# A wide last tile in a fused retention and feed-forward kernel, and a reserve of work kept back for it

## Chip, cores, metric

One core of one Trainium2 chip. The metric is device time in microseconds (us) of one execution; most executions of one kernel agree within 0.3%. TensorE is called PE, VectorE DVE, ScalarE ACT, GpSimd POOL; the queue that issues all DMAs here is SyncE's (SPq).

## The reference

```python
def _attn_ref(q, k, v):                  # q, k, v: (4, 8, 768, 64), float32
    gamma = 1.0 - 2.0 ** (-5.0 - np.arange(H))
    for t in range(S):
        state = gamma * state + outer(k[:, :, t], v[:, :, t])
        y[:, :, t] = q[:, :, t] @ state / sqrt(D)

def _moe_ref(x, w1, w2, w3, w_out):      # x: (3072, 512) from y; w1, w2: (512, 1024)
    a = x @ w1
    b = x @ w2
    return (a * b @ w3) @ w_out          # (3072, 512)
```

The kernel computes the first part in 24 steps of 128 tokens and multiplies w3 and w_out once, so that the second part is a product (a), a product (b), their elementwise product and one more product (O) for each tile of tokens.

## The kernel before

A step does the scores of its 128 tokens, the state, and the outputs. Between these, a queue of units of the feed-forward part fills PE. The key reaches a step in three moves: a load, a transpose by DMA (into kT), and two copies by ACT into the layout that the scores read (kp). A tile of 256 tokens gives 16 a and b units (4 matmuls of 256 columns each, 0.44 us) and two O units (8 matmuls of 512 columns, 1.73 us). Cuts are marked.

```python
        def a_unit(self, f, tag=None):
            ps = self.mm(W1, f, tag)                       # 4 matmuls into a PSUM buffer, one of 3
            self.pa[f] = fsb.tile([128, TB], FP, tag="pa", name="pa", bufs=5)
            nc.scalar.copy(self.pa[f][:, :], ps[:, :])     # ACT frees the buffer

        def b_unit(self, f):
            ...
            ps = self.mm(W2, f)
            nc.vector.tensor_tensor(                       # DVE frees the buffer, and needs pa
                self.HT[:, f : f + TB // self.width, :].rearrange("p f n -> p (f n)"),
                self.pa.pop(f)[:, :], ps[:, :], MULT,
            )
...
        for i in range(0, len(units), 8):                  # a b a b a b a b O a b a b a b a b O
            fill.units += units[i : i + 8] + late[:1]
            late = late[1:]
...
    def step(n):
        ready = n * C
        share = fill.available(ready) / (2 - n % 2)
        casts(n + 2)                                       # POOL, cut: only n >= 4
        scores(n)
        fill.pull(share * 0.25, ready)
        t_new = kv(n)
        dma_transposes(n + 2)
        load_chunk(n + 4)
        ...
        fill.pull(share * 0.25, ready)
        outputs(n)
        Tst[0] = t_new
        transposes(n + 1)                                  # two ACT copies of the key into kp
        fill.pull(share * 0.5, ready)
```

Loads, transposes by DMA and stores of the output are all issued on one in-order queue.

Of the kernel before, what the change touches and what calls it, by code (L numbers as in the profile page):

```python
# [9 lines left out]
FP = mybir.dt.float32  # L10
HP = mybir.dt.float16
AF = mybir.ActivationFunctionType
MULT = mybir.AluOpType.mult
# [5 lines left out]
def kernel(  # L19
# [11 lines left out]
    nc = tc.nc  # L31
    B, H, S, D = q.shape
    C = 128
    WST = 12
    NCH = S // C
    NSTEP = B * NCH
    NTOK = B * S
    DT0 = 6
    NP = H // 2
    DM = 512  # L40
# [7 lines left out]
    wstage = ctx.enter_context(tc.tile_pool(name="wstage", bufs=WST))  # L48
    xpool = ctx.enter_context(tc.tile_pool(name="xpool", bufs=4))
    ld = ctx.enter_context(tc.tile_pool(name="ld", bufs=6))  # L50
    att = ctx.enter_context(tc.tile_pool(name="att", bufs=2))
    fsb = ctx.enter_context(tc.tile_pool(name="fsb", bufs=2))
# [3 lines left out]
    ps_f = ctx.enter_context(tc.tile_pool(name="ps_f", bufs=3, space=PSUM))  # L56
# [154 lines left out]
    for h in range(H):  # L211
        p, r = h // 2, (h % 2) * 64
        nc.gpsimd.memset(GS[r : r + 64, p, r : r + 64], gam[h] ** C)

    XT = {}
# [6 lines left out]
    W3O = [wpool.tile([128, DM], HP, name=f"w3o_{i}") for i in range(8)]  # L222
# [19 lines left out]
    def bank(tag, shape, dtype, name):  # L242
        return (ps_t if tag == "psT" else ps_at).tile(shape, dtype, tag=tag, name=name)
# [89 lines left out]
    def casts(n):  # L333
        if n >= NSTEP:
            return
        k32, v32 = chunk_in.pop(n)
        if n % 2 == 0:
            q_cast(n // 2)
        k16 = att.tile([128, 512], HP, tag="k16", name="k16", bufs=3)
        nc.gpsimd.tensor_copy(k16[:, :], k32[:, :])  # L340
        vp = VP[n % 3]

        for r in range(2):
            nc.gpsimd.tensor_tensor(  # L344
                vp[:, :, r, r * 64 : r * 64 + 64],
                v32[:, :].rearrange("j (p s e) -> j p s e", s=2, e=64)[:, :, r, :],
                VS[:, :].rearrange("j (p s) -> j p s", s=2)[:, :, r].unsqueeze(2).broadcast_to((128, NP, 64)),
                MULT,
            )
        k16s[n] = k16  # L350

    def q_transposes(m, later=False):

        if m >= DT0 // 2:
            return
# [25 lines left out]
    def by_dma(n):  # L381

        return n >= DT0 and n != DT0 + 1

    def dma_transposes(n):

        if n < DT0 or n >= NSTEP:
            return
# [11 lines left out]
    def queries(n, p):  # L400
        if n < DT0:
            return qTs[n][:, p, :]
        c = n % 2
        return qTd[n // 2][:, :, p, c * 64 : (c + 1) * 64]
# [67 lines left out]
    def outputs(n, tag="psY"):  # L472
        am, vp = ATs.pop(n), VP[n % 3]
        c = n % NCH
        ps = bank(tag, [128, NP, 128], FP, "psY")
        for p in range(NP):
            nc.tensor.matmul(ps[:, p, :], lhsT=vp[:, p, 0, :], rhs=am[:, p, 0, :], start=True, stop=False)  # L477
            nc.tensor.matmul(ps[:, p, :], lhsT=vp[:, p, 1, :], rhs=am[:, p, 1, :], start=False, stop=(c == 0))  # L478
            if c > 0:
                nc.tensor.matmul(ps[:, p, :], lhsT=Tst[0][:, p, :], rhs=queries(n, p), start=False, stop=True)  # L480
        if n % 2 == 0:
            XT[n // 2] = xpool.tile([128, NP, 256], HP, tag="xt", name="xt")

        order = "p a (t i) -> p a t i"
        nc.vector.tensor_tensor(  # L485
            XT[n // 2][:, :, n % 2 * C : (n % 2 + 1) * C].rearrange("p a (i t) -> p a t i", t=2),
            ps[:, :, :].rearrange(order, t=2), YS[:, :, :].rearrange(order, t=2), MULT,
        )


    TB = 256

    class Ffn:
        def __init__(self, tok0, width):
            self.tok0, self.width = tok0, width
            self.HT, self.pa = None, {}

        def mm(self, W, f, tag=None):

            if tag:  # L500
                ps = bank(tag, [128, TB], FP, "psG")
            else:
                ps = ps_f.tile([128, TB], FP, tag="psF", name="psF")
            w, c0 = self.width, self.tok0 % TB
            m = TB // w
            for i in range(m):
                for d in range(4):
                    nc.tensor.matmul(  # L508
                        ps[:, i * w : (i + 1) * w], lhsT=W[d][:, (f + i) * 128 : (f + i + 1) * 128],
                        rhs=XT[self.tok0 // TB][:, d, c0 : c0 + w],  # L510
                        start=(i == 0 and d == 0), stop=(i == m - 1 and d == 3),
                    )
            return ps

        def a_unit(self, f, tag=None):
            ps = self.mm(W1, f, tag)
            self.pa[f] = fsb.tile([128, TB], FP, tag="pa", name="pa", bufs=5)
            nc.scalar.copy(self.pa[f][:, :], ps[:, :])  # L518

        def b_unit(self, f):  # L520
            if self.HT is None:
                self.HT = fsb.tile([128, 8, self.width], HP, tag="ht", name="ht", bufs=3)
            ps = self.mm(W2, f)
            nc.vector.tensor_tensor(  # L524
                self.HT[:, f : f + TB // self.width, :].rearrange("p f n -> p (f n)"),
                self.pa.pop(f)[:, :], ps[:, :], MULT,
            )

        def o_unit(self, tb, between=None):
            psO = ps_f.tile([128, DM], FP, tag="psF", name="psO")  # L530
            for f in range(8):
                if f == 4 and between:
                    between()
                nc.tensor.matmul(  # L534
                    psO[:, :], lhsT=self.HT[:, f, tb * 128 : (tb + 1) * 128], rhs=W3O[f][:, :],
                    start=(f == 0), stop=(f == 7),
                )
            osb = fsb.tile([128, DM], FP, tag="osb", name="osb", bufs=3)
            nc.scalar.activation(osb[:, :], psO[:, :], AF.Copy, scale=final_scale)  # L539
            r0 = self.tok0 + tb * 128  # L540
            nc.sync.dma_start(out[r0 : r0 + 128, :], osb[:, :])

        def last_o_unit(self, tb):

            osb = fsb.tile([128, DM], FP, tag="osb", name="osb", bufs=3)
            r0 = self.tok0 + tb * 128
            for c0, c1 in ((0, 320), (320, 512)):
                cs = slice(c0, c1)
                psO = ps_f.tile([128, c1 - c0], FP, tag="psF", name="psO")
                for f in range(8):  # L550
                    nc.tensor.matmul(
                        psO[:, :], lhsT=self.HT[:, f, tb * 128 : (tb + 1) * 128], rhs=W3O[f][:, cs],
                        start=(f == 0), stop=(f == 7),
                    )
                nc.scalar.activation(osb[:, cs], psO[:, :], AF.Copy, scale=final_scale)
                nc.sync.dma_start(out[r0 : r0 + 128, cs], osb[:, cs])

        def ab_units(self):
            need, m = self.tok0 + self.width, TB // self.width
            units = []  # L560
            for f in range(0, 8, m):
                units += [(need, 0.43, lambda f=f: self.a_unit(f)), (need, 0.43, lambda f=f: self.b_unit(f))]
            return units

        def o_units(self):
# [29 lines left out]

    fill = Queue()

    bounds = [0, 256] + list(range(384, 513, 128)) + list(range(768, NTOK + 1, 256))

    def step(n):  # L600

        ready = n * C
        share = fill.available(ready) / (2 - n % 2)
        if n >= DT0 - 2:
            casts(n + 2)
        scores(n)
        fill.pull(share * 0.25, ready)
        t_new = kv(n)
        if n < DT0 - 2:
            casts(n + 2)  # L610
        dma_transposes(n + 2)
        load_chunk(n + 4)
        if n % 2:
            q_transposes((n + 1) // 2)
        if n == 4:
            transposes(5)
        fill.pull(share * 0.25, ready)
        if n == 5:

            fill.units.pop(0)  # L620
            ffn[1].o_unit(0, lambda: [outputs(n), transposes(6)])
        else:
            outputs(n)
        Tst[0] = t_new
        if n not in (4, 5):
            transposes(n + 1)
        fill.pull(share * 0.5, ready)
# [79 lines left out]
    NT = len(ffn)  # L707
    f0 = ffn[0]
    hold = [new_stage() for _ in range(2)]
    f0.HT = fsb.tile([128, 8, TB], HP, tag="ht", name="ht", bufs=3)  # L710

    def four_banks(tags):
        got = []
# [16 lines left out]
    ps = four_banks(("psF", "psF", "psF", "psY"))  # L730
# [14 lines left out]
    pa = [hold[i // 2][:, i % 2 * 512 : i % 2 * 512 + 512].rearrange("p (a n) -> p a n", a=2) for i in range(4)]  # L745
# [12 lines left out]
    ps = four_banks(("psF", "psF", "psF", "psT"))  # L758
# [11 lines left out]
    by_rows(W2, ps, 3)  # L770
    f1.a_unit(4, "psK")
    for i in range(4):
        nc.vector.tensor_tensor(f0.HT[:, 2 * i : 2 * i + 2, :], pa[i], ps[i], MULT)  # L773
    outputs(3, "psA1")
    f1.a_unit(6, "psA0")
    casts(4)
# [4 lines left out]
    for t in range(1, NT):  # L781
        late = ffn[t - 1].o_units() if t > 1 else []
        units = ffn[t].ab_units()
        if t == 1:
            units = units[1::2]
# [46 lines left out]
```

## Time and profile before

| | before |
|---|---|
| time, median of 2 runs | 195.08 us (194.8 to 195.36) |
| span in the trace | 193.0 us, granted clock 1.00 |
| PE busy | 184.5 us (96%) |

The lines that carry it are in the prediction below: PE is full from about 45 us to its last matmul. One more count is used below, PE time lost: for each matmul the start of the next, less its own start, less its columns at 2.4 GHz plus 2.5 ns (109.2 ns for 256 columns; in the trace 32 of them take 3.493 us, 109.2 ns each); gaps over 20 ns are summed from 70 us of the span on, which leaves out the start. For the kernel before this sum is 0.0 us. The profile's own idle column shows less for the same gap, because a matmul's recorded end contains its latency (273 ns recorded for 256 columns, 109 ns from start to start).

### The profile page before, as it was taken

Reading aid. Unit: us, or ns where it says so; the run is one execution under the profiler, and the core shown is the slowest. Engines: PE = TensorE matmul, PEld = TensorE weight load, DVE = VectorE, ACT = ScalarE, POOL = GpSimd, SP = SyncE. Lnnn points to the kernel's source line nnn. Section 1 sums busy time; section 2 is a strip of 40 time slices with the busy share of each in tenths; the row PEclk is TensorE's granted clock in tenths of the full one; section 3 lists DMA queues with packets and bytes.
Section 4 is the critical chain, followed back from the end, with each engine's and each line's share of the span. In section 5 each row is a group of like instructions: output and inputs, shape, how many; then the busy total and the mean of one; then the engine's idle time right before and its main releaser. Section 6 shows DMA issues by size and latency. Waiting matters only on the chain.

```text
span 193.0 us, 4697 instructions
## 1 busy us (share of the span) xinstructions
PE 184.5 (96%) x1777; PEld 139.6 (72%) x1777; DVE 117.4 (61%) x220; ACT 99.5 (52%) x192; POOL 85.6 (44%) x146
## 2 busy tenths in 40 slices
PE   6789999789999999999999999999999999999993
PEld 2335667577797798777977797778777877887752
DVE  3227597699587758656665676565656665753220
ACT  6578555772454464454635463555355545533322
POOL 7600378638872658467152742863326432200000
PEclk9999999999999999999999999999999999999999
DMA  5999999999799999999999999979989930111104
GB/s 207 367 392 389 301 399 323 363 295 209 175 209 229 234 206 242 142 268 215 218 268 213 199 206 232 194 154 277 188 182 196 207 94 20 58 54 54 39 28 155
DMA packets 85030, 40.54 MB, mean 210 GB/s; under 512 B 61328, under 2 KB 80016, under 8 KB 85008
## 3 DMA queue, kind: packets, MB, share of 16 engines
q1 hardware_dynamic: 85008, 40.25, 88.9%
q8 instruction: 14, 0.23, 0.6%
q14 instruction: 8, 0.07, 0.1%
HBM read 29.36 MB, written 6.29 MB: 185 GB/s over the span
## 4 chain that ended last, share of the span: by engine, by line
PE 70%; DMA 17%; POOL 4%; DVE 3%; SPq 2%; issue 1%; ACT 1%; POOLq 0%; DVEq 0%; ACTq 0%
PE psF L508 36%; PE psO L534 18%; DMA stg<-in_v_dram 5%; DMA stg<-in_moe_w_dram 5%; PE psA L437 4%; DMA v<-in_v_dram 4%; DMA kT<-k 3%; SPq L62 2%; PE psY L477 2%; PE psY L478 2%; POOL vp L318 2%; PE psY L480 2%; PE psK L460 2%; PE psF L724 1%; DVE am L442 1%
## 5 line engine op out<-in xcount | busy, mean ns | idle before, releaser
L508 PE MATMUL psF<-xt,w 128*128 128x256 f16 (+1 forms) x736 | 85.0, 266 | 0.0
L508 PEld LDWEIGHTS <-w 128*128 128x128 f16 x768 | 68.2, 98 | 7.2
L524 DVE TENSOR_TENSOR ht<-pa,psF 128x256 f16<-128x256 f32 x88 | 36.5, 416 | 22.5 <-PE psF L508 12.9
L518 ACT COPY pa<-psF 128x256 f32<-128x256 f32 x84 | 31.2, 372 | 34.0 <-PE psF L508 33.5
L442 DVE TENSOR_TENSOR am<-psA,keep 128x512 f16<-128x512 f32 x48 | 31.0, 685 | 21.3 <-PE psA L437 21.2
L534 PE MATMUL psO<-w3o,ht 128*128 128x512 f16 x184 | 43.3, 379 | 0.0
L469 POOL TENSOR_TENSOR t<-s,GS 128x512 f16<-128x512 f32 x15 | 19.3, 1285 | 34.7 <-DVE s L468 34.7
L539 ACT ACTIVATE osb<-psO 128x512 f32<-128x512 f32 x23 | 13.7, 597 | 35.2 <-PE psO L534 35.2
L534 PEld LDWEIGHTS <-ht 128*128 128x128 f16 x184 | 17.8, 98 | 16.9 <-DVE ht L773 0.2
L344 POOL TENSOR_TENSOR vp<-v,VS 128x256 f16<-128x256 f32 x40 | 23.8, 615 | 8.9 <-DMA v<-in_v_dram 4.4
L327 POOL CAST q<-q 128x1024 f16<-128x1024 f32 x12 | 12.6, 1054 | 27.8 <-DMA q<-in_q_dram 27.8
L485 DVE TENSOR_TENSOR xt<-psY,YS 128x512 f16<-128x512 f32 x24 | 17.8, 743 | 4.0 <-PE psY L480 3.6
L477 PE MATMUL psY<-am,vp 128*128 128x128 f16 x96 | 16.8, 219 | 0.6 <-ACT kp L230 0.4
L478 PE MATMUL psY<-am,vp 128*128 128x128 f16 x96 | 16.7, 219 | 0.6 <-DVE vp L318 0.6
L437 PEld LDWEIGHTS <-kp 128*128 128x128 f16 x192 | 12.4, 98 | 5.2 <-DVE kp L228 0.4
L340 POOL CAST k<-k 128x512 f16<-128x512 f32 x20 | 12.2, 611 | 5.0 <-PE psK L460 3.6
L468 DVE TENSOR_TENSOR s<-psK,t 128x512 f32<-128x512 f32 x16 | 11.0, 688 | 3.0 <-PE psK L460 2.5
L411 ACT COPY kp<-kT 64x512 f16<-64x512 f16 x17 | 10.5, 618 | 2.5 <-DMA kT<-k 2.1
L251 DVE COPY w3t<-psW 128x1024 f16<-128x1024 f16 x8 | 5.5, 690 | 10.3 <-PE psW L259 7.9
L437 PE MATMUL psA<-qTd,kp 128*128 128x128 f16 x144 | 11.3, 219 | 0.1
L480 PE MATMUL psY<-qTd,t 128*128 128x128 f16 x60 | 10.8, 219 | 0.0
L412 ACT COPY kp<-kT 64x512 f16<-64x512 f16 x17 | 10.5, 615 | 0.4
(82 smaller groups left out, 190.4 us busy)
## 6 DMA issues: line engine op xcount, KB each, us to landing
stg<-in_moe_w_dram SPq DMA_DIRECT2D x16, 512.0 KB, 7.7
q<-in_q_dram SPq DMA_DIRECT2D x12, 512.0 KB, 5.6
out_dram<-osb SPq DMA_DIRECT2D x23, 256.0 KB, 3.1
k<-in_k_dram SPq DMA_DIRECT2D x20, 256.0 KB, 5.2
v<-in_v_dram SPq DMA_DIRECT2D x20, 256.0 KB, 5.5
stg<-in_moe_w_out_dram SPq DMA_DIRECT2D x4, 512.0 KB, 7.6
stg<-in_k_dram SPq DMA_DIRECT2D x2, 512.0 KB, 10.7
stg<-in_v_dram SPq DMA_DIRECT2D x2, 512.0 KB, 8.2
```

What stands on the lines that cost most here:

```text
L344: nc.gpsimd.tensor_tensor(vp[:, :, r, r * 64 : r * 64 + 64], v32[:, :].rearrange("j (p s e) -> j p s e", s=2, e=64)[:, :, r, :], VS[:, :]. ...
L437: nc.tensor.matmul(ps[:, i, r, :], lhsT=kp[:, p, r, :], rhs=queries(n, p), start=True, stop=True)
L442: nc.vector.tensor_tensor(am[:, half * 2 : half * 2 + 2, :, :].rearrange("j p s i -> j (p s) i"), ps[:, :, :, :].rearrange("j p s i -> j ( ...
L469: eng.tensor_tensor(t16[:, :, :], s32[:, :, :], GS[:, :, :], MULT)
L477: nc.tensor.matmul(ps[:, p, :], lhsT=vp[:, p, 0, :], rhs=am[:, p, 0, :], start=True, stop=False)
L478: nc.tensor.matmul(ps[:, p, :], lhsT=vp[:, p, 1, :], rhs=am[:, p, 1, :], start=False, stop=(c == 0))
L480: nc.tensor.matmul(ps[:, p, :], lhsT=Tst[0][:, p, :], rhs=queries(n, p), start=False, stop=True)
L485: nc.vector.tensor_tensor(XT[n // 2][:, :, n % 2 * C : (n % 2 + 1) * C].rearrange("p a (i t) -> p a t i", t=2), ps[:, :, :].rearrange(orde ...
L508: nc.tensor.matmul(ps[:, i * w : (i + 1) * w], lhsT=W[d][:, (f + i) * 128 : (f + i + 1) * 128], rhs=XT[self.tok0 // TB][:, d, c0 : c0 + w] ...
L518: nc.scalar.copy(self.pa[f][:, :], ps[:, :])
L524: nc.vector.tensor_tensor(self.HT[:, f : f + TB // self.width, :].rearrange("p f n -> p (f n)"), self.pa.pop(f)[:, :], ps[:, :], MULT,)
L534: nc.tensor.matmul(psO[:, :], lhsT=self.HT[:, f, tb * 128 : (tb + 1) * 128], rhs=W3O[f][:, :], start=(f == 0), stop=(f == 7),)
```

## The change

Intent: the last 512 tokens become one tile with matmuls of 512 columns. That tile can start only when step 23 is done, so steps 20 to 23 would lack work; a tile's worth of units (10.3 us by the kernel's own cost figures) is kept back, growing over steps 8 to 19. The diff, cut to its core (the rest names buffers by width):

```diff
+    WIDE = 20
...
-        if n % 2 == 0:
-            XT[n // 2] = xpool.tile([128, NP, 256], HP, tag="xt", name="xt")
+        w = 4 if n >= WIDE else 2
+        if n % w == 0:
+            pool, tag = (wstage, "wst") if w == 4 else (xpool, "xt")
+            XT[n // w * w] = pool.tile([128, NP, w * C], HP, tag=tag, name="xt")
...
-                ps = ps_f.tile([128, TB], FP, tag="psF", name="psF")
+                ps = ps_f.tile([128, m * w], FP, tag="psF", name="psF")
...
+            return [wstage.tile([128, 4, self.width], HP, tag="wst", name="ht") for _ in range(2)]
...
-            self.pa[f] = fsb.tile([128, TB], FP, tag="pa", name="pa", bufs=5)
+            self.pa[f] = fsb.tile([128, self.m * self.width], FP, tag="pa", name="pa", bufs=4)
...
-    bounds = [0, 256] + list(range(384, 513, 128)) + list(range(768, NTOK + 1, 256))
+    bounds = [0, 256] + list(range(384, 513, 128)) + list(range(768, WIDE * C, 256))
+    bounds += list(range(WIDE * C, NTOK + 1, 512))
+    RES = 10.3
...
-        share = fill.available(ready) / (2 - n % 2)
+        if n >= WIDE:
+            share = fill.available(ready) / (4 - n % 4)
+        else:
+            keep_back = RES * max(0, n - 7) / (WIDE - 8)
+            share = max(0.0, fill.available(ready) - keep_back) / (2 - n % 2)
```

More of the change, by code (lines that the diff above doesn't have):

```diff
@@ L480, in outputs @@
                 nc.tensor.matmul(ps[:, p, :], lhsT=Tst[0][:, p, :], rhs=queries(n, p), start=False, stop=True)
-        if n % 2 == 0:
-            XT[n // 2] = xpool.tile([128, NP, 256], HP, tag="xt", name="xt")
+        w = 4 if n >= WIDE else 2
+        if n % w == 0:
+            pool, tag = (wstage, "wst") if w == 4 else (xpool, "xt")
+            XT[n // w * w] = pool.tile([128, NP, w * C], HP, tag=tag, name="xt")
+        c0 = n % w * C
         order = "p a (t i) -> p a t i"
         nc.vector.tensor_tensor(
-            XT[n // 2][:, :, n % 2 * C : (n % 2 + 1) * C].rearrange("p a (i t) -> p a t i", t=2),
+            XT[n // w * w][:, :, c0 : c0 + C].rearrange("p a (i t) -> p a t i", t=2),
             ps[:, :, :].rearrange(order, t=2), YS[:, :, :].rearrange(order, t=2), MULT,
@@ L495, in __init__ @@
             self.tok0, self.width = tok0, width
+            self.m = max(1, TB // width)
             self.HT, self.pa = None, {}
         def mm(self, W, f, tag=None):
+            w, m = self.width, self.m
+            x0 = self.tok0 // max(w, TB) * max(w, TB)
+            c0 = self.tok0 - x0
             if tag:
-                ps = bank(tag, [128, TB], FP, "psG")
+                ps = bank(tag, [128, m * w], FP, "psG")
             else:
-                ps = ps_f.tile([128, TB], FP, tag="psF", name="psF")
-            w, c0 = self.width, self.tok0 % TB
-            m = TB // w
+                ps = ps_f.tile([128, m * w], FP, tag="psF", name="psF")
             for i in range(m):
@@ L509, in mm @@
                         ps[:, i * w : (i + 1) * w], lhsT=W[d][:, (f + i) * 128 : (f + i + 1) * 128],
-                        rhs=XT[self.tok0 // TB][:, d, c0 : c0 + w],
+                        rhs=XT[x0 // C][:, d, c0 : c0 + w],
                         start=(i == 0 and d == 0), stop=(i == m - 1 and d == 3),
@@ L513, in mm, with new_ht, ht @@
             return ps
+        def new_ht(self):
+            if self.width <= TB:
+                return [fsb.tile([128, 8, self.width], HP, tag="ht", name="ht", bufs=3)]
+            return [wstage.tile([128, 4, self.width], HP, tag="wst", name="ht") for _ in range(2)]
+        def ht(self, a, b):
+            n = 8 // len(self.HT)
+            return self.HT[a // n][:, a % n : (b - 1) % n + 1, :]
         def a_unit(self, f, tag=None):
             ps = self.mm(W1, f, tag)
-            self.pa[f] = fsb.tile([128, TB], FP, tag="pa", name="pa", bufs=5)
+            self.pa[f] = fsb.tile([128, self.m * self.width], FP, tag="pa", name="pa", bufs=4)
             nc.scalar.copy(self.pa[f][:, :], ps[:, :])
@@ L521, in b_unit @@
             if self.HT is None:
-                self.HT = fsb.tile([128, 8, self.width], HP, tag="ht", name="ht", bufs=3)
+                self.HT = self.new_ht()
             ps = self.mm(W2, f)
             nc.vector.tensor_tensor(
-                self.HT[:, f : f + TB // self.width, :].rearrange("p f n -> p (f n)"),
+                self.ht(f, f + self.m).rearrange("p f n -> p (f n)"),
                 self.pa.pop(f)[:, :], ps[:, :], MULT,
@@ L534, in o_unit @@
                 nc.tensor.matmul(
-                    psO[:, :], lhsT=self.HT[:, f, tb * 128 : (tb + 1) * 128], rhs=W3O[f][:, :],
+                    psO[:, :], lhsT=self.ht(f, f + 1)[:, 0, tb * 128 : (tb + 1) * 128], rhs=W3O[f][:, :],
                     start=(f == 0), stop=(f == 7),
@@ L551, in last_o_unit @@
                     nc.tensor.matmul(
-                        psO[:, :], lhsT=self.HT[:, f, tb * 128 : (tb + 1) * 128], rhs=W3O[f][:, cs],
+                        psO[:, :], lhsT=self.ht(f, f + 1)[:, 0, tb * 128 : (tb + 1) * 128], rhs=W3O[f][:, cs],
                         start=(f == 0), stop=(f == 7),
@@ L558, in ab_units @@
         def ab_units(self):
-            need, m = self.tok0 + self.width, TB // self.width
+            need, m = self.tok0 + self.width, self.m
+            cost = 0.43 * m * self.width / TB
             units = []
             for f in range(0, 8, m):
-                units += [(need, 0.43, lambda f=f: self.a_unit(f)), (need, 0.43, lambda f=f: self.b_unit(f))]
+                units += [(need, cost, lambda f=f: self.a_unit(f)), (need, cost, lambda f=f: self.b_unit(f))]
             return units
@@ L709 @@
     hold = [new_stage() for _ in range(2)]
-    f0.HT = fsb.tile([128, 8, TB], HP, tag="ht", name="ht", bufs=3)
+    f0.HT = f0.new_ht()
     def four_banks(tags):
@@ L772 @@
     for i in range(4):
-        nc.vector.tensor_tensor(f0.HT[:, 2 * i : 2 * i + 2, :], pa[i], ps[i], MULT)
+        nc.vector.tensor_tensor(f0.ht(2 * i, 2 * i + 2), pa[i], ps[i], MULT)
     outputs(3, "psA1")
```

## The prediction

> **What bounds the kernel now.** I read first the page's busy shares and its slices, then the busy time by stretches, then the chain in order of time, then the matmuls by form, and last the DMA's side (the waits, the timelines of GpSimd and of the issuing queue).
>
> ```profile
> PE 184.5 (96%) x1777; PEld 139.6 (72%) x1777; DVE 117.4 (61%) x220; ACT 99.5 (52%) x192; POOL 85.6 (44%) x146
> ...
> PE   6789999789999999999999999999999999999993
> ...
> DMA  5999999999799999999999999979989930111104
> ```
>
> TensorE is full from about 45 us to the last slice. The DMA row is as full until about 155 us and then almost empty: the kernel loads and computes at the same rate up to step 19 and only computes after that. The stretches say it in numbers (us; then busy time of PE, weight loads, VectorE, ScalarE, GpSimd; clock; DMA share; GB/s):
>
> ```profile
> 80.00:100.00 20.00, 20.00 (x196) 16.03 (x195) 12.60 (x25) 10.13 (x22) 11.16 (x15) 1.00 1.24 234
> ...
> 170.00:180.00 10.00, 10.00 (x93) 8.10 (x90) 5.11 (x11) 3.93 (x10) 0.00 (x0) 1.00 0.14 52
> 180.00:193.00 13.00, 10.08 (x71) 6.58 (x69) 1.87 (x5) 3.94 (x9) 0.00 (x0) 1.00 0.23 82
> ```
>
> No PE idle is left in the stretches that the change rearranges; the idle 2.9 us of the last one are the last copy and store. The chain that ended last is accordingly PE for the whole tail, unit after unit:
>
> ```profile
> 176.17 3.49 PE psF L508 x32
> 179.66 1.73 PE psO L534 x8
> 181.39 3.49 PE psF L508 x32
> 184.88 3.45 PE psO L534 x16
> 188.34 1.76 PE psO L551 x16
> ```
>
> This gives the pace of issue: 32 matmuls of 256 columns in 3.49 us are 109.1 ns each, 16 of 512 columns in 3.45 us are 215.6 ns each. (The groups print 273 and 379 ns, which are latencies of overlapping instructions.)
>
> **What the Trainium skill says.** (1) "TensorE: Matmul & The Clock Gate", Part 1, "Wait — 56ns, not 53.3ns?": a warm back-to-back matmul starts every N / 2.4 GHz plus about 2.5 ns: 109.2 ns at 256 columns, 215.8 at 512. The trace agrees (109.1, 215.6). So a wide matmul saves only that fixed 2.5 ns against two narrow ones. (2) The same page, Part 2, step 1: weight loads are pulled ahead and run beside matmuls. The trace agrees: PEld is 8 us busy of 10 while PE is never idle, so halving the weight loads frees nothing. (3) "PSUM — Partial Sum Buffer", "The four PSUM rules": one matmul's output is at most one bank, 512 fp32. So a 512-wide unit just fits a bank; the three psF buffers remain three; the 512-column fp32 psO tiles of this trace are of that size. (4) "DMA: Bandwidth & Descriptors", Specifications: under 512 B a transfer is below line rate. The page of before counts 61328 of 85030 packets under 512 B, and it moves 200 to 234 GB/s with full engines in the middle against up to 399 GB/s in slices with large weight loads. So I take the DMA as nearly full in steps 8 to 19, though what is in reserve has to be read from this trace.
>
> **The change, part by part.**
>
> *The wide tile.* Tokens 2560 to 3071 were two tiles, each with 8 features x 4 x 2 weights = 64 matmuls of 256 columns; they become 64 of 512. The built programs' order confirms 696 against 568 matmuls of 256 columns and 261 against 325 of 512, all others equal. Cost: 128 x 109.1 = 13.97 us against 64 x 215.6 = 13.80 us: **-0.17 us** on a bound engine, so it counts.
>
> *Copies and products.* Sixteen of 128x256 on ScalarE (372 ns) become 8 of 128x512 (about 597 ns, from the output copy of that shape), sixteen products on VectorE (416 ns) become 8 of about 690 ns (from the mask product 685 and the output product 743 of that shape). A wide unit takes PE 4 x 215.6 = 0.86 us, so a pair takes PE 1.72 us, VectorE 0.7, ScalarE 0.6. Neither becomes the bound, and with three PSUM buffers each has a whole other unit's time. Worth 0. The two output units of the tile before, placed after the 8th and the 16th unit, still cover the last product before the first own output unit.
>
> *The last tile needs all of steps 20 to 23.* Before, half of its work ran in steps 22 and 23. Now none can, so something else must fill them: the reserve. The program of after has in steps 8 to 19 324 narrow matmuls and 10 output units, before 12 x 32 = 384 and 12. Kept back: 60 x 0.109 + 2 x 1.73 = 10.0 us. Steps 20 to 23 then hold 124 narrow ones and four output units, before 128 and four. So these steps keep their length, and behind step 23 stand 13.8 us of wide units and six output units (10.4 us). PE's sum is the same: work moved from steps 8-19 to the end, 10 us, at no cost if the steps shortened by it stay full.
>
> *Can steps 8 to 19 be shortened?* In the trace a step is 6.56 us (scores at 150.0, 156.6, 163.1): 5.22 us of filler and 1.34 of its own. Now they average 6.56 - 10.0 / 12 = 5.7 us, a pair 11.4 us. The other engines in such a step: VectorE 2 x 0.69 + 0.69 + 0.74 + 4 x 0.83 x 0.42 = 4.2 us; GpSimd 0.53 + 0.61 + 1.19 + 1.28 = 3.6 us. Both fit. The DMA:
>
> ```profile
> 72.63 1.04 POOL L327 CAST q<-q 128x1024 f16<-128x1024 f32 x1 [1.76 <-DMA q<-in_q_dram]
> ...
> 83.94 1.04 POOL L327 CAST q<-q 128x1024 f16<-128x1024 f32 x1 [0.92 <-DMA q<-in_q_dram]
> ...
> 95.80 1.04 POOL L327 CAST q<-q 128x1024 f16<-128x1024 f32 x1 [4.20 <-DMA q<-in_q_dram]
> ...
> 108.75 1.04 POOL L327 CAST q<-q 128x1024 f16<-128x1024 f32 x1
> ```
>
> Up to 95.8 us the cast starts when its load lands: the loads come as fast as they can, a pair every 11.1 us (the k loads of chunks 8 and 14 land at 63.6 and 96.9 us: 33.3 / 3). From 108.75 on nothing waits: PE's 13 us per pair have let the loads get ahead. The queue that issues them then has idle time of its own (about 1.3 to 1.8 us in a pair, waiting for an output), and there are two outputs fewer in these steps. So supply is **11.1 us a pair against a demand of 11.4**. Step by step, with the transposed k's landing in the trace before plus 1.25 us for its two copies: ready at 82.4, 88.8, 94.2, 100.4, 104.0 us for steps 10 to 14; by the new order PE wants them at 83.2, 89.7, 94.7, 100.6, 105.9. All are in time, by 0.2 to 1.9 us. For steps 15 on the old landings would be up to 1 us late, but those were held back by outputs that PE had not yet produced, which now come sooner. I book **+0.3 us** for one or two slips.
>
> Sum: 195.08 - 0.17 + 0.3 = 195.2 us.
>
> **Rivals.** *A: the DMA becomes the bound in steps 8 to 19.* For it: margins of 0.2 to 0.8 us, and pairs in the trace that took 11.8 and 12.2 us. At 11.8, six pairs lose 6 x 0.4 = 2.4 us, 197.5 us; at 12.2, 6 x 0.8 = 4.8 us, 199.9 us, slower by over 2%; a PE that idles long enough could lose clock as well, though the granted clock was 1.00 throughout before. Against: the 12.2 pair was one in which the queue waited for an output, and steps 20 to 23 are as long as before, so what is late there is forgiven. *B: thinner cover inside a step.* Between scores and outputs the masking needs about 1.7 us from the first score; steps 9 and 15 now have there 12 narrow matmuls and the state's 4, 12 x 0.109 + 0.22 = 1.53 us after 0.44 us of scores, 2.0 us. It holds by 0.3 us if VectorE is free, and an output unit runs just before, so it is. If it fails, 0.2 us in a few steps: 195.6 us. *C: the wide tile is worth more.* If narrow matmuls suffered stalls that wide ones don't, the tail would shrink; the tail shows 109.1 ns in unbroken rows, so there is nothing of that kind: 194.9 us at best. A gain over 2% (3.9 us) has no idle time to come from.
>
> **Range and chances.** The middle is 195.2 us. Below, only the 0.17 us and the spread of the runs (194.8 to 195.36): low 194.3. Above, a half of rival A: high 197.0. Faster 0.01, same 0.95, slower 0.04, which is A in full.
>
> **What would show it.** Right: PE 9 in all slices as before; rows of 512 columns at 0.216 us each in the tail; scores of step 20 near 140 us instead of 150; the DMA row empty some 10 us earlier; the same PE end within 0.5 us. Wrong: PE idle before scores of steps 9 to 19 released by the copies of the transposed k (which wait for its DMA), PE slices of 8 between 80 and 140 us, and the loads' pair period over 11.4 us.

## The result, and the profile after

| | before | after |
|---|---|---|
| time, median of 2 runs each | 195.08 us | 197.76 us (197.62 to 197.91) |
| ratio | | 1.014, 95% interval 1.0105 to 1.0174 |
| span in the trace | 193.0 us | 195.9 us |
| PE time lost from 70 us on | 0.0 us | 3.01 us |

The time is within 2%, slower clear of noise, and 0.76 us above the range predicted.

The page of after, the same rows as shown of before:

```profile
PE 185.0 (94%) x1713; PEld 133.5 (68%) x1713; DVE 114.7 (59%) x212; ACT 97.7 (50%) x184; POOL 86.1 (44%) x146
...
PE   6789999789999999999999999799999999999993
...
DMA  6999999999899999999999999999999111101024
```

The DMA row empties a slice earlier: the last transposed key lands at 152.8 us instead of 160.2, 7.4 us earlier. PE has a 7 in the middle. The stretches:

```profile
80.00:100.00 20.00, 19.37 (x191) 15.31 (x190) 13.19 (x26) 10.08 (x22) 11.12 (x15) 1.00 1.16 224
...
120.00:140.00 20.00, 18.29 (x179) 14.65 (x178) 11.27 (x23) 9.28 (x21) 9.07 (x14) 1.00 1.22 209
```

PE idles in two stretches of the part with the reserve, while the clock is 1.00 in both. The tail, in the chain of time, is as predicted:

```profile
168.71 6.91 PE psF L514 x32
175.62 1.73 PE psO L549 x8
177.34 6.91 PE psF L514 x32
184.25 6.91 PE psO L549 x32
```

By the unrounded starts 32 matmuls of 512 columns take 6.907 us, 215.8 ns each, where two rows of 32 narrow ones took 2 x 3.493 = 6.986 us. The wide tile gains 0.08 us a row, 0.16 us in both. So the loss is before the tail. PE's waits after 60 us, released by what, sum, times, longest (before has no such line):

```profile
PE psF L514 <- ACT pa L533: 2.3, 4, 1.3
```

Four waits are all of it: a fill unit waits for ACT to copy an a unit and so free its PSUM buffer. By the count of starts they are 0.42 us at the end of step 10, 0.54 in step 11, 1.50 in step 16 and 0.53 in step 17, 2.99 us of the 3.01. Less the wide tile's 0.16 us that makes +2.8 us; the spans differ by 2.9. Step 20 begins at 143.0 us, not at 150.0 as before and not at the 140.0 that the units' sum gives.

Two of the four have a late key in them. ACT and PE in step 16, in order of time (start, duration, engine, line, what; in brackets the idle before and its releaser):

```profile
120.80 0.60 ACT L554 ACTIVATE osb<-psO 128x512 f32<-128x512 f32 x1 [2.46 <-PE psO L549]
121.29 0.37 ACT L533 COPY pa<-psF 128x256 f32<-128x256 f32 x1
...
121.70 1.91 PE L514 MATMUL psF<-xt,w 128*128 128x256 f16 x16
123.26 0.62 ACT L412 COPY kp<-kT 64x512 f16<-64x512 f16 x1 [1.60 <-DMA kT<-k]
...
123.89 0.62 ACT L413 COPY kp<-kT 64x512 f16<-64x512 f16 x1
124.53 0.65 ACT L533 COPY pa<-psF 128x256 f32<-128x256 f32 x2
...
124.95 0.60 PE L514 MATMUL psF<-xt,w 128*128 128x256 f16 x4 [1.34 <-ACT pa L533]
```

ACT stands 1.60 us before its key copy, for a DMA; a product that PE finished meanwhile waits behind it, and PE waits for that. The scores that need the key come after. In all, ACT waited 3.7 us for keys after 60 us of the span, against 0.4 us before. In step 11 no DMA is late (that key landed at 91.0 us):

```profile
92.91 0.60 ACT L554 ACTIVATE osb<-psO 128x512 f32<-128x512 f32 x1 [2.24 <-PE psO L549]
...
93.38 1.47 PE L514 MATMUL psF<-xt,w 128*128 128x256 f16 x12
93.53 0.62 ACT L412 COPY kp<-kT 64x512 f16<-64x512 f16 x1
94.16 0.61 ACT L413 COPY kp<-kT 64x512 f16<-64x512 f16 x1
94.80 0.65 ACT L533 COPY pa<-psF 128x256 f32<-128x256 f32 x2
...
95.22 0.60 PE L514 MATMUL psF<-xt,w 128*128 128x256 f16 x4 [0.37 <-ACT pa L533]
```

ACT never idles from 92.91 on: output copy, two key copies, then the copy that PE needs. PE's 12 matmuls, three units, take 12 x 0.109 = 1.31 us from 93.38; the fourth unit could start at 94.69 and starts at 95.22: 0.53 us lost (0.54 by the unrounded starts). The Trainium skill has it in "TensorE: Matmul & The Clock Gate", specification table, "Engine queue depth": ACT and DVE are strict FIFO. The trace of step 16 agrees: the first a unit of the 16 matmuls was done at 122.74 us by its last matmul's recorded end, but its copy began at 124.53 us, behind a key copy whose DMA had not landed before 123.24 us.

It helps to write a step's PE order as letters (read from the built program): S scores, k state, | outputs, a, b, O the units.

```
step      before           after
 10     Sabakbab|abO     SbkOa|bababa
 11     Sababab|abO      SbO|abab
 16     Sabakbab|abO     SbkOa|babab
 17     Sababab|abO      SabO|abab
```

Before, every step from 8 to 23 ends in "abO": while ACT does the key copies, PE has an a, a b and the long O, which just fill the three buffers and last 2.6 us. The reserve broke that phase.

From this come two theories. **Supply**: at steps of 5.7 us the queue delivers keys too late. **Order**: units in the wrong places behind the outputs run PE out of buffers while ACT is busy.

### The profile page after: what moved, and what is told of

Read it like the earlier page. It is cut to its first block, busy times and chain, and to the rows that moved or that the text cites. A ratio compares the mean times of both kernels' runs of the same rounds, so it can differ in the third digit from the quotient of the medians.

```text
span 195.9 us, 4536 instructions
## 1 busy us (share of the span) xinstructions
PE 185.0 (94%) x1713; PEld 133.5 (68%) x1713; DVE 114.7 (59%) x212; ACT 97.7 (50%) x184; POOL 86.1 (44%) x146
## 4 chain that ended last, share of the span: by engine, by line
PE 70%; DMA 17%; ACT 5%; issue 3%; DVE 1%; SPq 1%; POOL 1%; ACTq 0%; DVEq 0%; POOLq 0%
PE psF L514 34%; PE psO L549 19%; DMA stg<-in_moe_w_dram 6%; DMA q<-in_q_dram 5%; DMA kT<-k 4%; PE psA L438 4%; DMA stg<-in_moe_w_out_dram 3%; PE psY L478 2%; PE psY L479 2%; PE psK L461 2%; PE psY L481 2%; ACT kp L413 2%; ACT pa L533 1%; PE psF L748 1%; SPq L63 1%
## 5 line engine op out<-in xcount | busy, mean ns | idle before, releaser
L514 PE MATMUL psF<-xt,w 128*128 128x256 f16 (+2 forms) x672 | 85.5, 275 | 2.3 <-ACT pa L533 2.3
L514 PEld LDWEIGHTS <-w 128*128 128x128 f16 x704 | 62.2, 98 | 17.0 <-issue 3.0
L539 DVE TENSOR_TENSOR ht<-pa,psF 128x256 f16<-128x256 f32 (+1 forms) x80 | 35.2, 442 | 31.3 <-PE psF L514 18.6
L533 ACT COPY pa<-psF 128x256 f32<-128x256 f32 (+1 forms) x76 | 29.6, 395 | 36.5 <-PE psF L514 36.2
L443 DVE TENSOR_TENSOR am<-psA,keep 128x512 f16<-128x512 f32 x48 | 30.9, 684 | 10.3 <-PE psA L438 9.9
L412 ACT COPY kp<-kT 64x512 f16<-64x512 f16 x17 | 10.5, 618 | 4.5 <-DMA kT<-k 4.2
L438 PE MATMUL psA<-qTd,kp 128*128 128x128 f16 x144 | 11.1, 219 | 0.0
L479 PEld LDWEIGHTS <-vp 128*128 128x128 f16 x96 | 9.4, 98 | 1.8 <-POOL vp L319 1.0
```

Of the source, the lines that this page charges most:

```text
L438: nc.tensor.matmul(ps[:, i, r, :], lhsT=kp[:, p, r, :], rhs=queries(n, p), start=True, stop=True)
L443: nc.vector.tensor_tensor(am[:, half * 2 : half * 2 + 2, :, :].rearrange("j p s i -> j (p s) i"), ps[:, :, :, :].rearrange("j p s i -> j ( ...
L479: nc.tensor.matmul(ps[:, p, :], lhsT=vp[:, p, 1, :], rhs=am[:, p, 1, :], start=False, stop=(c == 0))
L514: nc.tensor.matmul(ps[:, i * w : (i + 1) * w], lhsT=W[d][:, (f + i) * 128 : (f + i + 1) * 128], rhs=XT[x0 // C][:, d, c0 : c0 + w], start= ...
L539: nc.vector.tensor_tensor(self.ht(f, f + self.m).rearrange("p f n -> p (f n)"), self.pa.pop(f)[:, :], ps[:, :], MULT,)
```

## The experiments

Time lost is PE's, from 70 us on, in the one trace of each run; times are medians, and so is the time of before beside it.

| run | time, before beside it | ratio (95%) | PE lost in its trace |
|---|---|---|---|
| reserve_only | 198.66, 195.38 | 1.0185 (1.0157-1.0213) | 3.41 |
| light_loads (wrong) | 195.7, 195.38 | 1.0022 (1.0007-1.0037) | 1.08 |
| outputs_last | 196.94, 195.38 | 1.0074 (1.002-1.0128) | 1.33 |
| four_banks | 196.15, 195.38 | 1.0045 (1.0006-1.0085) | 2.14 |
| light_last (wrong) | 194.89, 194.81 | 0.9995 (0.9969-1.0022) | 0.19 |
| even_reserve | 195.8, 194.81 | 1.0044 (1.0014-1.0073) | 0.99 |
| late_stores | 197.24, 194.81 | 1.0136 (1.0095-1.0178) | 1.76 |
| late_stores_last | 196.14, 194.81 | 1.0044 (1.0011-1.0078) | 0.19 |
| after_again | 197.29, 195.02 | 1.0124 (1.0094-1.0154) | 1.86 |
| outputs_early | 196.94, 195.02 | 1.0092 (1.0072-1.0112) | 1.90 |
| key_copy_split | 196.89, 195.02 | 1.0097 (1.0071-1.0123) | 1.75 |
| wide_only | 195.57, 195.02 | 1.0027 (1.0002-1.0051) | 0.74 |
| copy_first | 203.73, 195.23 | 1.0442 (1.0414-1.047) | 8.67 |
| small_reserve | 194.72, 195.23 | 0.9982 (0.9961-1.0004) | 0.00 |

In the diffs below, `...` marks cuts, and remarks behind # are added here. The traced run is not always a typical one: it was the fastest of its runs for even_reserve, late_stores and after_again, and the slowest for four_banks.

### reserve_only: which half of the change costs

```diff
-        w = 4 if n >= WIDE else 2
+        w = 2
...
-    bounds = [0, 256] + list(range(384, 513, 128)) + list(range(768, WIDE * C, 256))
-    bounds += list(range(WIDE * C, NTOK + 1, 512))
+    bounds = [0, 256] + list(range(384, 513, 128)) + list(range(768, NTOK + 1, 256))
```

> The reserve alone, with the last 512 tokens as two tiles of 256 as before. If the loss comes from the reserve (the four PE stalls at the end of steps 10, 11, 16 and 17, 2.99 us in the trace of after), this is as slow as the change: 197.9 us, ratio to before 1.014 to 1.016, the same four stalls. If the wide tile costs it (its copies, its larger buffers), this is as fast as before: 195.1 us.

198.66 us against 195.38. The stalls of steps 11, 16 and 17 are there with 0.54, 1.55 and 0.54 us; that of step 10 is missing, and step 22, whose filler the new tile bounds changed, has 0.54 and 0.22 us. The reserve costs; the wide tile doesn't.

### light_loads: less to load, same order

```diff
         for nm, src in (("k", k), ("v", v)):
+            if nm == "v" and n >= 10:
+                tiles.append(V9[0])          # chunk 9's v again: wrong on purpose
+                continue
...
```

> The change, with the loads of v dropped from chunk 10 on (a wrong result on purpose): a quarter of the bytes of q, k and v less, all else the same order. Theory of supply (the DMA is too slow for steps of 5.7 us): the transposed k's land earlier and all of the loss goes, 195.0 us. Theory of order (without an output unit behind the outputs, the fill runs out of its three PSUM buffers while ScalarE does its output copy and the two key copies first): the stalls of steps 11 and 17, where the key had long landed, stay at 0.53 us each; those of 10 and 16 shrink to 0 to 0.5 each; 196.0 to 196.9 us.

195.7 us, a little faster than the range for two causes (196.0 to 196.9) and clearly not the 195.0 of supply alone. Its PE waits:

```profile
PE psF L519 <- ACT pa L538: 0.8, 2, 0.4
```

Two are left, 0.54 us each, at steps 11 and 17; those of 10 and 16 are gone, and ACT no longer waits for any key after 60 us. (From chunk 10 on v is a third of the bytes of q, k and v, not the quarter that the expectation says.) So the 1.08 us at steps 11 and 17 has nothing to do with loads, and the 1.92 us of steps 10 and 16 has.

### outputs_last: same units in each step, O at its end

```diff
+        8: (3, 3, 2, 1), 9: (2, 2, 3, 0), 10: (3, 3, 2, 1), 11: (2, 2, 1, 1), ...
-        fill.pull(share * 0.25, ready)       # and likewise behind kv and behind outputs
+        fill.ab(plan[0], ready)              # a/b units before kv, before outputs, after; then O
```

> The change, with the same number of narrow units and output units in each of steps 8 to 19, but inside a step the output unit always last, as the kernel before has it. Theory of order: PE finds 1.73 us of work that needs one PSUM buffer while ScalarE does the key copies; the stalls of steps 10, 11, 16, 17 go, 194.9 to 195.4 us. Theory of supply: the same bytes at the same pace, so PE waits as long, now before the scores: 197.3 to 198 us.

196.94 us, with single runs from 195.41 to 197.47: between the two. The profiled run lost 0.19 us at step 11 by order and 1.14 us at the scores of steps 17 and 19, with the key copies as releasers:

```profile
PE psA L438 <- ACT kp L413: 0.4, 1, 0.4
```

The order part went and the supply part became visible as what it is, a key that comes too late for its scores. In these two traces order also set what a late key costs: here ACT stood 2.73 us for the key of step 17, and PE lost 0.86 us by it; in after it stood 1.60 us, and PE lost 1.50.

### four_banks: a fourth PSUM buffer

```diff
+        if now[0] >= 8 and turn[0] % 4 == 0:
+            return ps_t.tile(shape, FP, tag="psT", name=name)   # idle from step 8 on
```

> The change, with a fourth PSUM buffer for the fill units from step 8 on (a bank that stands idle by then). Theory of order: each stall shrinks by the 0.44 us of one more narrow unit: 11 and 17 to 0.1, 10 to 0, 16 to 1.06; sum 1.2 instead of 3.0, 196.0 us. Theory of supply alone: the scores still wait for the late key, 197.3 to 197.8 us.

196.15 us, near the 196.0 of order, but the sum was right by luck: the profiled run lost 2.14 us, and 1.66 us of these at the scores of steps 14, 17 and 19, which waited for keys and once (step 14) for queries. With more buffers PE runs further ahead and then meets the late key itself.

### light_last: both causes taken away

The edits of light_loads and outputs_last together.

> Both repairs at once, a wrong result on purpose: no v loads from chunk 10 on, and the output unit last in its step. If order (1.08 us in light_loads, at steps 11 and 17) and supply (the rest, at steps 10 and 16) make up the whole loss, no PE stall over 0.1 us is left after 60 us and the time is 194.9 to 195.3 us, the time of before less 0.17. If a third cause is there, about 0.5 to 1 us of loss stays.

194.89 us against 194.81, and one gap of 0.19 us left. No third cause of any size is there.

### even_reserve: the same reserve, spread over all 16 steps

```diff
+    PLAN = {n: (2, 3, 2, int(n not in (16, 23))) for n in range(8, 24)}   # a/b, a/b, a/b, O
+    for n in (11, 17, 23):
+        PLAN[n] = (5, 0) + PLAN[n][2:]
...
```

> A right result: the reserve spread evenly, each of steps 8 to 23 takes seven narrow units and, but for two of them, one output unit, placed last. A pair of steps then takes 11.9 to 12.3 us instead of 11.4. Theory of supply (the queue delivers a pair in 11.1 to 11.8 us) together with order: no stall, 194.9 to 195.3 us, no faster than before by more than 0.17. If the loads can't deliver even this, PE waits before scores and it stays at 196 to 197.5 as outputs_last.

195.8 us: better than the change, not level with before, and between the two forecasts. In its trace the scores of step 17 lost 0.31 us, but not to a late load: that key had landed at 121.66 us, and its copies began at 124.01 us, straight behind a copy of an a unit. They came too late for PE because step 16 has no O unit to cover them. The rest are four gaps of 0.12 to 0.19 us. ACT waited for no key after 60 us, so the loads keep this pace in the traced run, the fastest of six; what the slower ones lost isn't known.

### late_stores and late_stores_last: stores behind loads in the queue

In the trace of after, the key of step 17 was issued at 118.06 us, right behind a store whose issue took 2.63 us.

```diff
-            nc.sync.dma_start(out[r0 : r0 + 128, :], osb[:, :])
+            send(out[r0 : r0 + 128, :], osb[:, :])   # in steps 8 to 19: held.append((dst, src))
...
         load_chunk(n + 4)
+        send_held()
```

> The change, but in steps 8 to 19 an output's store is issued behind the next step's transposes and loads instead of before them; same bytes, same PE order. If the late key of step 17 (and of step 11) was held up by the store at the head of the one in-order queue (2.63 us of issue at 115.33 us), these land earlier, the stall of step 16 goes from 1.50 to under 0.5, and 1.1 us remains at steps 11 and 17: 196.0 to 196.6 us. If the bytes are the limit, the order in the queue changes nothing: 197.3 to 198 us.

> A right result: stores behind the loads and output units last in their step. If order and the head of the queue are all of it, 194.9 to 195.3 us. If the bytes are the limit, the 0.5 to 1.4 us that outputs_last still loses stay: 195.8 to 197.4 us.

late_stores: 197.24 us, as if nothing had changed, though its profiled run (196.53 us) shows the stall of step 16 gone, 0.53 us each left at steps 11 and 17, and a new 0.70 us at step 18. late_stores_last: 196.14 us, with runs from 194.68 to 196.65; its profiled run (196.43 us) lost 0.19 us from step 8 on, but had begun late: the scores of step 6 at 62.1 us instead of 60.4. In these traces late keys stand at other steps than in after, but the second trace of the unedited change, below, has other sizes too, so the place of the store isn't shown as the reason; and the trace of one run doesn't tell what the slower runs lost. Whether bytes or places in the queue make keys late stays open.

### after_again: the change once more

```diff
-    RES = 10.3
+    RES = 10.3  # again
```

> The change itself once more, word for word, beside the others of this call and for a second trace. The stalls of steps 11 and 17 (order) should be the same 0.53 us each in the second trace to within 0.02; those that come from late keys may move to other steps and sizes. Time 197.4 to 198.3 us.

197.29 us (196.73 to 198.06), just under the forecast. Steps 11 and 17 lost 0.53 us each, as in the first trace. Step 10 lost nothing and step 16 0.80 us instead of 1.50. The order's part is fixed, the keys' part varies from run to run.

### outputs_early and copy_first: order alone, at the pace of before

Both start from the kernel before, without reserve or wide tile.

```diff
+            fill.ab(3, ready)      # outputs_early; 2 in copy_first
...
+            fill.o()               # in front of outputs
...
+            fill.ab(5, ready)      # outputs_early; 6 in copy_first
```

In letters a step is SabakO|babab in the first, SabkO|ababab in the second.

> The kernel before, no reserve, narrow tiles, same units in each step, but in steps 8 to 23 the output unit stands in front of the outputs and five narrow units behind them. The pace and the loads are those of before, so by the theory of supply alone nothing is lost: 195.1 us. By the theory of order each of these 16 steps gets the stall of steps 11 and 17, 0.53 us: 8.5 us in sum, 203.6 us; if fewer steps have it (VectorE and ScalarE catching up), at least 4 us.

> As outputs_early (the kernel before, no reserve, the output unit in front of the outputs in steps 8 to 23), but with two narrow units in front and six behind, so that the first unit behind the outputs is one whose copy ScalarE makes (a) and not one whose product VectorE makes (b). outputs_early lost 0.10 us a step and the change 0.53 us at its steps 11 and 17; if what tells them apart is which kind comes first (a blocked copy holds its own buffer and that of the product that needs it, so PE gets one unit of 0.44 us less far), each step here loses 0.53 us, 16 x 0.53 = 8.5 us, 203.5 us, with loads and pace no tighter than before. If the 0.53 us needs the short steps of the reserve, it stays near 196.9 us as outputs_early.

outputs_early: 196.94 us; the forecast by order was far too high. Each of steps 8 to 22 lost (step 23 has no key copies behind it), but 0.10 us (0.32 in steps 12 and 18, whose outputs have 8 matmuls instead of 12, so that PE comes to the units 0.22 us sooner), not 0.53. copy_first: 203.73 us, 0.53 to 0.54 us in each of steps 8 to 22 (0.76 in those two), 8.67 us in sum; loads and pace were those of before or easier. One of them, in order of time:

```profile
89.88 0.60 ACT L539 ACTIVATE osb<-psO 128x512 f32<-128x512 f32 x1 [2.01 <-PE psO L534]
...
90.35 1.47 PE L508 MATMUL psF<-xt,w 128*128 128x256 f16 x12
90.50 0.62 ACT L411 COPY kp<-kT 64x512 f16<-64x512 f16 x1
...
91.13 0.61 ACT L412 COPY kp<-kT 64x512 f16<-64x512 f16 x1
...
91.77 0.65 ACT L518 COPY pa<-psF 128x256 f32<-128x256 f32 x2
...
92.20 1.05 PE L508 MATMUL psF<-xt,w 128*128 128x256 f16 x8 [0.37 <-ACT pa L518]
```

It is step 11 of the change over again. The buffers explain the difference. With "abab", the first a holds a buffer that only ACT frees, the b behind it holds one that DVE can't free without that copy, the third unit takes the buffer that the O unit left, and the fourth has none: PE gets three units, 1.31 us. With "babab", DVE frees the first b's buffer at once, since its a was copied before the key copies: four units, 1.75 us. The difference is one unit, 0.437 us, and 0.535 - 0.437 = 0.098 us is what outputs_early lost. The change also has four buffers for the copies of a units (pa) instead of five; that isn't the cause, since these two runs keep five and stall, and small_reserve has four and doesn't.

### key_copy_split: the second key copy on DVE

```diff
-            nc.scalar.copy(kp[64:128, :, 1, :], kT[64:128, :, :])
+            nc.vector.tensor_copy(kp[64:128, :, 1, :], kT[64:128, :, :])
```

> The change, with the second of the two key copies of a step on VectorE instead of ScalarE. ScalarE then has 0.62 us less in front of the copies that free PSUM. Theory of order: the stalls of 0.53 us at steps 11 and 17 go; those behind late keys shrink by about 0.4 each; 195.6 to 196.6 us, unless VectorE, waiting for the key in its turn, holds up products as ScalarE did copies: then 197 to 198.

196.89 us. The stalls of steps 11 and 17 went as expected, but steps 9, 10 and 15 have 0.19 us each, step 14 has 0.25, and step 16 still loses 0.94 us, half of it now to a product of DVE that stood behind the late key. The burst (the copies that ACT has to do in a row) was moved, not removed.

### wide_only and small_reserve: how much reserve is needed

```diff
-    RES = 10.3
+    RES = 0.0
+    PLAN = {18: (3, 3, 1, 1), 19: (3, 3, 1, 1), 20: (2, 1, 3, 0),      # small_reserve only
+            21: (2, 1, 0, 1), 22: (2, 1, 3, 0), 23: (3, 0, 0, 1)}
```

> The wide tile with no reserve: steps 8 to 19 as before, steps 20 to 23 have half the filler, 2.6 us each. If steps so thin could be run full, the reserve would be needless and this would be 194.9 us. I expect them to be bound by the step's own chain (scores, mask 1.7 us, outputs, keys' copies), 0.5 to 1 us idle in each: 197 to 199 us, PE idle in steps 20 to 23 alone and none in steps 8 to 19.

> A right result: the wide tile with a reserve of two narrow units alone, kept back in steps 18 and 19, where the keys land 6 us early, and laid where wide_only still idled (steps 21 and 23); output units last or, where a step is thin, straight behind the outputs. If order and supply are all, no stall over 0.1 us and 194.85 us, the time of before less 0.17; if thin steps have a bound of their own, 195.4 to 196 us.

wide_only: 195.57 us. I had expected 197 to 199: steps with half the filler lost 0.74 us in all, 0.10 in step 21 and 0.64 in step 23, where too few units cover the mask. small_reserve moves two narrow units, 0.87 us, out of steps 18 and 19 and lays them where wide_only idled: 194.72 us, no gap at all. From the scores of step 8 (72.19 us; before 72.16) to the start of the last matmul (189.70 us; before 189.84) it takes 0.16 us less: the gain of the wide tile and nothing else. Against before the ratio is 0.9982 with an interval that contains 1, so it is level in time; that it is faster is seen in the traces, not shown by the times.

## Why the prediction was wrong, point by point

- **The bound and the tail: right.** PE is the bound; the wide rows ran at 215.8 ns a matmul (215.6 used), and the tail gained 0.16 us (0.17 predicted).
- **The copies and products at double width: right.** Nothing in the tail waits for them, and reserve_only loses as much without them.
- **The reserve as work moved "at no cost if the steps shortened by it stay full": the condition failed**, by 2.99 us in the first trace. The term booked for it, **"+0.3 us for one or two slips"**, is the one that was mis-sized. What it stood for measured 1.92 us in the steps with a late key (10 and 16; 0.80 in the second trace) and 1.07 us by order alone (11 and 17, the same in both).
- **Late keys: the mechanism was named, in rival A, and too little was given to it.** The list of margins compared each key with the moment when PE wants the scores. But the key copies stand in ACT's line in front of the copies that free PSUM, so PE feels a late key already at the end of the step before. For step 11 the list had 88.8 us against 89.7, in time by 0.9; in the run the key landed at 87.5 us (87.4 before), and ACT was kept 0.52 us by it. (The list's times are 0.1 to 0.2 us later than the landings plus 1.25 us; nothing hangs on that.) Of steps 15 on the prediction said that the keys had been held back by outputs "which now come sooner". The key of step 17, whose stall is the largest, was indeed issued 2.07 us sooner (at 118.06 us, not 120.13), but took 5.18 us to land instead of 3.60: it came at 123.24 us, only 0.49 us sooner:

```profile
118.06 5.18 DMA kT<-k
```

  The idle time of the issuing queue, which the prediction counted as reserve, was used up: between 84 and 140 us of the span it was 8.0 us before, and in after no gap reaches 0.12 us. In after, the casts of q wait for their loads much longer than before, where the waiting ended at 95.80 us:

```profile
95.36 1.04 POOL L328 CAST q<-q 128x1024 f16<-128x1024 f32 x1 [3.58 <-DMA q<-in_q_dram]
...
106.33 1.04 POOL L328 CAST q<-q 128x1024 f16<-128x1024 f32 x1 [0.71 <-DMA q<-in_q_dram]
...
118.42 1.04 POOL L328 CAST q<-q 128x1024 f16<-128x1024 f32 x1 [1.39 <-DMA q<-in_q_dram]
...
129.43 1.04 POOL L328 CAST q<-q 128x1024 f16<-128x1024 f32 x1 [2.53 <-DMA q<-in_q_dram]
```

  That is a pair in (129.43 - 95.36) / 3 = 11.4 us, the demand itself and not 11.1, so no lead was built up.
- **Order: not foreseen.** Rival B looked at thin cover between scores and outputs; none of the four stalls is there. The cover that failed is the one behind the outputs, and the printed order of units, which was read for counts, showed it: "O|abab".
- **What would show it wrong:** the stated sign was PE idle before the scores of steps 9 to 19. All four stalls of after stand one or two units earlier, before fill units. PE slices of 8 (here a 7) did come. Of the signs for right, the rows of the tail came; the scores of step 20 came at 143.0 us, not near 140, and the DMA row emptied 7.4 us earlier, not 10.
- **The range:** half of rival A alone would have contained late keys of 1.9 us; with order's 1.1 on top the time ended 0.76 us outside. How far outside is partly luck: after_again's median is 0.29 us outside, and one of its four runs, 196.73 us, lies inside.

## What to carry to other kernels

Filler that keeps the busiest engine full has an order as well as an amount: which unit stands where another engine does a burst decides how many buffers are blocked, and a queue that hands units out by cost loses that phase when its amounts change. When a step is shortened on an engine without idle time, follow a late operand to the first in-order queue it blocks, not only to its own use. And measure the gap a reserve is meant to fill first: here it was 0.74 us, and 10 us were kept back for it.

## What the Trainium skill lacked or had wrong

- "TensorE: Matmul & The Clock Gate", Part 1: the fixed cost of about 2.5 ns a matmul held (109.2 ns at 256 columns, 215.8 at 512). Nothing to mend.
- The same page states the strict FIFO of ACT and DVE, and "PSUM — Partial Sum Buffer", "Engine vs sequencer instructions", repeats it; neither says what it means for PSUM buffers: with three buffers, the kind of the first unit behind a burst on ACT decided between 0.10 and 0.53 us lost in each step.
- "DMA: Bandwidth & Descriptors", Specifications, calls 512 B the least for line rate, but has no rate for a mix like this one. Here packets of 256 and 512 B with transposes and stores came to 209 to 230 GB/s with the engines full, and a pair of steps in 11.4 us.
- The same page, "Back-pressure in remote DMA", speaks of remote transfers alone; no page gives what an issue costs behind others on one core: a store's issue took 2.63 us in the trace of after, where the issuing queue had no idle time, and 0.36 us in that of before, where it had been idle.
